# A retention and phase-mixing kernel: a new written-out order with 40 DMA transposes for 35, and output tiles in token-weight buffers

## The chip, the cores and the metric

The kernel runs on one core of a Trainium2 chip. The metric is device time in microseconds, lower is better. The core has TensorE (PE, matrix products, with PEld for its weight loads), VectorE (DVE), ScalarE (ACT), GpSimd (POOL) and SyncE (SP), which here only issues transfers. ACT issues some too.

## The reference

The first half is a recurrent retention over 4 batches, 8 heads, 768 tokens and head size 64; the second mixes the result over tokens with a learned phase. Cut to what is computed:

```
state = gamma[h] * state + outer(k[t], v[t])          # per batch and head
x[t]  = scale * q[t] @ state                          # heads side by side: [4, 768, 512]
theta = x @ w_theta
y     = w_tok_r @ (x * cos(theta)) + w_tok_i @ (x * sin(theta))
u     = x + y
out   = u + relu(u @ w_ch)
```

All inputs and the output are float32; the products are done in bf16.

## The kernel before

Tokens are taken in *units*: unit n is 256 tokens of one batch and four of the eight heads, so 24 units, six to a batch. A *chunk* C is 128 tokens with all heads: 24 chunks, six to a batch. An output *tile* t is 128 tokens of the output.

Nothing is scheduled by a compiler. The string ORDER (L23) lists every step, and each engine executes its own steps in the order in which they stand there. SP has one queue for nearly all transfers, also in order. A step that waits therefore holds all that is behind it on its engine. The last letter of a token names the engine (p POOL, v DVE, a ACT) or the issuing queue (s SP, a ACT).

Per unit n: Lk, Lq and Lv (L157) load k, q and v, 256 KB each, into nine rotating buffers per kind. ck (L275) casts k, cq (L278) scales q by its decay, cv (L282) scales v. Then k and q are transposed into kqT, either on PE (Tk and Tq, L293, copied out of PSUM by E, L302), or by one DMA transpose Dk (L307). G(n) on PE is three groups: A(n) (scores of unit n, L323), Y(n-1) (scores times v, L393) and ST(n) (the new part of the state, L351). m(n) on DVE (L330) masks the scores. SU(n) on DVE (L357) updates the state, SB(n,g) (L369) copies half of it to bf16, and I(n) on PE (L375) multiplies q by it. So G(n), SU(n), SB(n), I(n), G(n+1) is a chain, and I(n) also waits until XA(n-1) on ACT (L409) has read the previous result out of the one PSUM buffer R.

Per chunk C: x is put in token order by Tx on PE (L424, copied by Ex) or by a DMA transpose Dx (L433); Hh on PE (L438) gives theta, CN on ACT (L445) cosine and sine, z (L451) their products with x. z of the six chunks of a batch and the transposed token weights are what the token mixing M(t,s0) on PE (L483, twelve matmuls to a tile) needs. The token weights come as twelve rows: Lw loads (four buffers "wtok", L184), cw casts, Tw transposes on PE (L469), Ew copies. The weights of theta and of the channel product come by Lth and Lch and are cast in four parts (cth, cch).

Per tile t: u on DVE (L492) adds x; u is transposed on PE (Tu, L497, copied by Eu) or by DMA (Du, L508); O on PE (L512) is the channel product; f on DVE (L519) the rectifier and the sum, into one of four "ot" buffers; SO (L524) stores it. A buffer of "ot" is free again when its store has landed. The last tile is done in two halves (Mh, uh, Tuh, Oh, fh, SOh). warm(n) puts n matmuls on PE whose result nobody reads (L255).

Of the kernel before, what the change touches and what calls it, by code (L numbers as in the profile page):

```python
# [14 lines left out]
FT = mybir.dt.float32  # L15
# [17 lines left out]
I.4 CN.1.0 Tx.3 ck.6.a G.5 cq.6.v Tq.6 Lv.7.s Lk.8.s CN.1.1 Lq.8.s z.0.p SU.5 SB.5.1.p Tk.6
cw.1.0.p cv.6.p Lw.0.1.s m.5 Lv.8.s Ex.3.a XA.4.1 Hh.3 XA.4.0 ck.7.p Tx.2 cq.7.p Lk.9.s E.6.v
Lq.9.s Hh.2 Ex.2.v CN.3.0 ck.8.p SB.5.0.a z.1.v Lw.1.1.s Tw.1.0 Lv.9.s Ew.1.0.v CN.3.1 cq.8.p I.5
cv.7.p CN.2.0 z.3.v cv.8.p G.6 XA.5.1 Tk.7 XA.5.0 Hh.5 Lk.10.s Tq.7 Tk.8 CN.2.1 m.6 CN.5.1 Lq.10.s
CN.5.0 SU.6 Hh.4 E.7.v SB.6.1.a Tq.8 SB.6.0.a Tx.4 M.0.0 I.6 cw.0.1.a G.7 z.2.v E.8.v Ex.4.v Tx.5
SU.7 CN.4.1 Lw.0.2.s M.0.1 Ex.5.v ck.9.p CN.4.0 cq.9.p M.0.2 XA.6.0 Tw.0.1 SB.7.1.p XA.6.1
SB.7.0.a Lw.1.2.s m.7 z.4.v Tk.9 M.0.3 Tq.9 Ew.0.1.a cw.1.1.p I.7 Lv.10.s Lk.11.s G.8 XA.7.0
Lq.11.s z.5.v E.9.a cv.9.p Tw.1.1 M.0.4 Ew.1.1.v XA.7.1 Lw.0.3.s M.0.5 u.0 Lw.1.3.s SU.8 SB.8.0.v  # L40
Hh.6 ck.10.p cq.10.p cw.0.2.p m.8 Lw.0.4.s cw.1.2.p Tk.10 Lw.1.4.s M.1.0 Lv.11.s M.1.1 CN.6.0
cw.0.3.p M.1.2 M.1.3 Tq.10 SB.8.1.a I.8 M.1.4 Tw.0.2 M.1.5 E.10.v Lch.s cw.1.3.p Lk.12.s Lq.12.s
Ew.0.2.v Tw.1.2 CN.6.1 cv.11.p G.9 Ew.1.2.a ck.11.a Hh.7 u.1 M.2.0 ck.12.p XA.8.0 CN.7.0 CN.7.1
M.2.1 cq.11.v cq.12.p cv.10.v SU.9 Lv.12.s Lk.13.s Tk.11 XA.8.1 SB.9.1.v M.2.2 Tq.11 cv.12.p M.2.3
M.2.4 SB.9.0.v ck.13.p Tw.0.3 Dx.6 Lw.0.5.s Lw.1.5.s m.9 M.2.5 Dk.12 E.11.a Tw.1.3 I.9 Lq.13.s
Lv.13.s cw.0.5.p Ew.0.3.v G.10 Lk.14.s Lq.14.s Ew.1.3.a Tu.0 u.2 SU.10 Eu.0.v M.3.0 M.3.1
SB.10.0.a Tu.1 cw.0.4.a cw.1.4.v Lv.14.s Lk.15.s Eu.1.v SB.10.1.v M.3.2 XA.9.0 m.10 M.3.3 cch.3.v
Tx.7 XA.9.1 cq.13.p M.3.4 Ex.7.a M.3.5 Tw.1.4 I.10 Tw.0.4 cch.1.a cch.0.a Dk.13 G.11 Ew.1.4.v
cch.2.v u.3 Tu.2 O.0 SU.11 Ew.0.4.a ck.14.p Tu.3 cv.14.p XA.10.0 M.4.0 Eu.2.a m.11 M.4.1 f.0
Eu.3.v z.6.v M.4.2 M.4.3 Lq.15.s SB.11.0.a O.1 M.4.4 cq.14.p XA.10.1 SB.11.1.a M.4.5 Tw.0.5 f.1  # L50
Lv.15.s Tx.8 Hh.8 Lk.16.s cw.1.5.a Ew.0.5.v I.11 Tw.1.5 u.4 Ex.8.a G.12 Ew.1.5.v Tx.9 M.5.0
Lq.16.s cq.15.p SU.12 M.5.1 z.7.v Ex.9.v Dk.14 CN.8.1 CN.8.0 XA.11.1 Hh.9 SB.12.1.v CN.9.0 Lv.16.s
ck.16.p O.2 XA.11.0 CN.9.1 z.8.v M.5.2 f.2 Lk.17.s M.5.3 Tx.11 M.5.4 Lq.17.s Lv.17.s SB.12.0.a
SO.0.s Ex.11.a M.5.5 Tx.10 Lk.18.s Hh.10 SO.1.s Hh.11 z.9.v cv.13.v SO.2.s Lq.18.s CN.10.0 ck.15.p
Lv.18.s u.5 M.6.0 m.12 M.6.1 CN.10.1 M.6.2 cv.15.p CN.11.1 cq.16.p Ex.10.v I.12 G.13 CN.11.0 M.6.3
z.10.v Tu.5 XA.12.1 z.11.v Eu.5.a M.6.4 SU.13 M.6.5 SB.13.0.v O.3 u.6 Tu.4 M.7.0 ck.17.p M.7.1
# [12 lines left out]
M.12.3 Lv.22.s Ex.17.v CN.16.1 XA.18.1 CN.17.0 m.19 SB.19.1.a z.16.v CN.17.1 O.9 I.19 SO.6.s G.20
M.12.4 z.17.v M.12.5 f.9 Lk.23.s XA.19.1 Hh.19 Lq.23.s Dk.22 O.10 SU.20 Lv.23.s cv.22.p u.12  # L70
M.14.0 SB.20.0.a m.20 M.14.1 CN.19.0 ck.23.p M.14.2 SB.20.1.v M.14.3 M.14.4 XA.19.0 cv.21.v
cq.23.p M.14.5 I.20 f.10 G.21 O.11 u.14 M.16.0 M.16.1 SU.21 M.16.2 Dx.18 XA.20.1 SB.21.0.a cv.23.p
XA.20.0 M.16.3 M.16.4 M.16.5 SB.21.1.v f.11 CN.19.1 m.21 Hh.18 I.21 u.16 Dk.23 M.15.0 M.15.1 Dx.19
Du.12 CN.18.1 SO.9.a G.22 M.15.2 SU.22 XA.21.0 SB.22.0.v XA.21.1 m.22 M.15.3 M.15.4 Du.16 SO.8.s
M.15.5 CN.18.0 Dx.20 Hh.21 u.15 SB.22.1.p I.22 G.23 XA.22.1 z.18.v M.13.0 z.19.p M.13.1 SU.23 m.23
SO.10.a Hh.20 XA.22.0 SB.23.0.v Dx.21 M.13.2 Du.14 M.13.3 M.13.4 M.20.0 CN.20.1 M.20.1 CN.20.0
CN.21.1 SB.23.1.v O.16 I.23 G.24 XA.23.0 f.16 M.13.5 XA.23.1 CN.21.0 z.20.p O.12 Hh.23 M.22.0 f.12
Hh.22 M.22.1 Dx.22 z.21.p CN.23.0 u.13 Dx.23 M.18.0 CN.22.0 SO.11.s M.22.2 CN.22.1 Du.15 M.18.1
M.20.2 z.22.v M.22.3 CN.23.1 M.18.2 M.18.3 M.22.4 z.23.v O.14 M.20.3 M.22.5 f.14 M.18.4 M.18.5
Du.13 M.20.4 u.22 u.18 M.19.0 O.15 M.17.0 M.19.1 SO.16.a M.17.1 f.15 SO.14.s M.19.2 Du.22 M.19.3  # L80
M.17.2 M.17.3 O.13 f.13 M.17.4 M.17.5 u.17 M.19.4 SO.12.s Du.18 O.18 M.21.0 M.21.1 f.18 M.19.5
O.22 u.19 Du.17 M.21.2 M.21.3 f.22 SO.15.s M.21.4 Du.19 SO.13.a M.21.5 u.21 Du.21 O.17 M.20.5 f.17
Mh.0.0 u.20 Mh.0.1 Mh.1.0 Mh.0.2 Mh.0.3 SO.18.a Mh.0.4 Mh.0.5 uh.0 O.19 Tu.20 Mh.1.1 SO.22.s f.19
Mh.1.2 Eu.20.a Mh.1.3 Mh.1.4 Mh.1.5 uh.1 SO.17.s Tuh.0 O.20 Euh.0 f.20 Tuh.1 O.21 SO.19.s Euh.1
Oh.0 Oh.1 f.21 SO.20.a SO.21.a fh.0 SOh.0 fh.1 SOh.1
""".split()


# [11 lines left out]
def kernel(  # L100
# [14 lines left out]
    B, H, S, D = q.shape  # L115
    dm = H * D
    P = 128
# [10 lines left out]
    io = ctx.enter_context(tc.tile_pool(name="io", bufs=2))  # L128
    work = ctx.enter_context(tc.tile_pool(name="work", bufs=3))
# [131 lines left out]
    st = {}  # L261
# [255 lines left out]
        st["o", t] = o_ps  # L517

    def f(t):  # L519
        st["ot", t] = work.tile([P, dm], FT, name="ot", bufs=4)  # L520
        nc.vector.scalar_tensor_tensor(st["ot", t], st["o", t], 0.0, st["u", t], ALU.max,  # L521
                                       ALU.add)

# [86 lines left out]
```

## Time and profile before

| | us |
|---|---|
| median of three runs | 170.73 |
| lowest and highest | 168.94, 171.44 |
| the profiled execution | 170.49 |
| its span | 168.8 |
| PE busy, ACT busy, POOL busy | 156.0, 79.2, 78.5 |
| DVE busy | 123.8 |
| matmuls for x transposes on PE (L427) | 52 |
| matmuls for u transposes on PE (L500) | 36 |
| DMA transposes (Dk, Dx, Du) | 10, 11, 14 |
| their median time from issue to landing | 4.7, 3.4, 3.3 |
| stores issued by SP and by ACT (whole tiles) | 16, 7 |
| HBM read, written | 25.69 MB, 6.29 MB |

How to read it: the slices cut the span in 40 parts of 4.2 us and show each engine's busy share in tenths. The groups give, for a line, engine and operation, the count, the busy time, the mean of one in ns, and the idle time of the engine before them with what ended it. Matmuls are pipelined, so the busy time of one is longer than the distance between two starts. The waits of SP's queue are times in which SP could not issue its next transfer.

### The profile page before, as it was taken

To read this page: it belongs to the slowest core of one execution; us is meant where nothing else is said; L and a number is where in the kernel's file an instruction comes from. 1 tells how busy PE (TensorE), PEld (TensorE's weight loads), DVE (VectorE), ACT (ScalarE), POOL (GpSimd) and SP (SyncE) were. 2 spreads that over 40 slices of the span, in tenths; PEclk is the share of its full clock that TensorE was granted. 3 is DMA by queue.
4 is the path that set the end of the run, shared out by engine and by line. 5 is a ranking of instruction groups with operands and counts; after the bars stand their busy time and mean duration, and the time that the engine had idled before them with its cause. 6 is when DMAs were issued, how large, how long until landed. Compare 5 with 4: busy or idle time off the path is not lost.

```text
span 168.8 us, 4924 instructions
## 1 busy us (share of the span) xinstructions
PE 156.0 (92%) x2017; PEld 89.0 (53%) x2044; DVE 123.8 (73%) x200; ACT 79.2 (47%) x159; POOL 78.5 (47%) x99
## 2 busy tenths in 40 slices
PE   7988794989899989999999999999999999999991
PEld 2555463557566655555645565554555444444660
DVE  3497979699999897899669979689737443526552
ACT  6346385587657755666322593674323544000030
POOL 3778377998932634669203658023354560000000
PEclk9999999599999999999999999999999999999999
DMA  4999999999799999999999188899998736335555
GB/s 141 296 290 332 329 322 289 274 319 350 257 283 329 221 232 292 254 207 309 305 244 227 65 188 209 124 276 168 269 230 133 197 62 186 93 93 194 88 188 186
DMA packets 68582, 38.20 MB, mean 226 GB/s; under 512 B 25936, under 2 KB 63056, under 8 KB 68560
## 3 DMA queue, kind: packets, MB, share of 16 engines
q1 hardware_dynamic: 67408, 35.92, 88.8%
q10 hardware_dynamic: 1152, 1.97, 3.5%
q8 instruction: 16, 0.26, 0.6%
q14 instruction: 6, 0.05, 0.1%
HBM read 25.69 MB, written 6.29 MB: 189 GB/s over the span
## 4 chain that ended last, share of the span: by engine, by line
PE 65%; DVE 14%; SPq 11%; DMA 4%; issue 2%; ACT 1%; DVEq 0%; ACTq 0%
PE y_ps L488 31%; PE o_ps L515 11%; PE th_ps L441 9%; SPq L157 9%; DVE z L455 5%; DMA qf<-in_q_dram 4%; DVE at L332 3%; PE at_ps L323 3%; PE r_ps L393 2%; PE r_ps L380 2%; PE y_ps L538 2%; DVE kqb L279 1%; PE kq_ps L293 1%; PE w_ps L472 1%; SPq L185 1%
## 5 line engine op out<-in xcount | busy, mean ns | idle before, releaser
L488 PE MATMUL y_ps<-z,wtr 128*128 128x512 bf16 x135 | 51.2, 379 | 1.0 <-DVE z L455 0.5
L488 PE MATMUL y_ps<-z,wti 128*128 128x512 bf16 x129 | 48.9, 379 | 0.4 <-issue 0.3
L413 ACT CAST xT<-r_ps 128x256 bf16<-128x256 f32 x48 | 16.9, 372 | 30.7 <-PE r_ps L351 19.6
L279 POOL TENSOR_TENSOR kqb<-qf,qsc 128x512 bf16<-128x512 f32 x20 | 23.7, 1189 | 14.1 <-DMA qf<-in_q_dram 13.7
L332 DVE TENSOR_TENSOR at<-at_ps,mask 128x1024 bf16<-128x1024 f32 x24 | 29.1, 1213 | 1.1 <-PE at_ps L323 1.0
L521 DVE SCALAR_TENSOR_TENSOR ot<-o_ps,u 128x512 f32<-128x512 f32 x23 | 15.8, 689 | 14.9 <-PE o_ps L515 14.8
L441 PE MATMUL th_ps<-wth,xT 128*128 128x512 bf16 x89 | 25.0, 395 | 1.4 <-POOL wth L139 1.0
L285 POOL TENSOR_TENSOR vb<-vf,vsc 128x512 bf16<-128x512 f32 x17 | 18.9, 1114 | 10.0 <-DMA vf<-in_v_dram 9.9
L515 PE MATMUL o_ps<-wch,uT 128*128 128x512 bf16 x88 | 23.2, 379 | 0.4 <-DVE wch L139 0.2
L488 PEld LDWEIGHTS <-wti 128*128 128x128 bf16 x138 | 13.5, 98 | 13.4 <-issue 1.1
L448 ACT ACTIVATE cs<-th_ps,halfpi 128x512 bf16<-128x512 f32 x24 | 16.5, 688 | 8.2 <-PE th_ps L441 5.8
L488 PEld LDWEIGHTS <-wtr 128*128 128x128 bf16 x138 | 13.5, 98 | 13.0
L495 DVE TENSOR_TENSOR u<-y_ps,x_sb 128x512 bf16<-128x512 f32 x23 | 15.8, 686 | 5.8 <-PE y_ps L488 5.8
L448 ACT ACTIVATE cs<-th_ps,zerob 128x512 bf16<-128x512 f32 x24 | 16.2, 687 | 5.7 <-PE th_ps L441 5.3
L455 DVE TENSOR_TENSOR z<-cs,x_sb 128x1024 bf16<-128x1024 bf16 x18 | 16.6, 936 | 2.9 <-ACT cs L448 2.7
L455 POOL TENSOR_TENSOR z<-cs,x_sb 128x1024 bf16<-128x1024 bf16 x6 | 12.9, 2153 | 6.6 <-DMA x_sb<-xT 3.9
L139 POOL CAST kqb<-kf 128x512 bf16<-128x512 f32 x16 | 10.6, 666 | 8.3 <-DMA kf<-in_k_dram 6.1
L441 PEld LDWEIGHTS <-xT 128*128 128x128 bf16 x96 | 9.0, 100 | 10.3 <-issue 1.8
L515 PEld LDWEIGHTS <-uT 128*128 128x128 bf16 x92 | 8.7, 98 | 9.5 <-issue 0.3
L137 ACT COPY uT<-u_ps 128x512 bf16<-128x512 bf16 x6 | 3.5, 589 | 21.3 <-PE u_ps L500 21.3
L258 PE MATMUL y_ps<-zero 128*128 128x512 bf16 x36 | 12.0, 447 | 1.4 <-DVE zero L194 1.3
L293 PE MATMUL kq_ps<-ident,kqb 128*128 128x128 bf16 x112 | 9.8, 223 | 2.2 <-DVE kqb L279 2.2
(74 smaller groups left out, 209.3 us busy)
## 6 DMA issues: line engine op xcount, KB each, us to landing
kf<-in_k_dram SPq DMA_DIRECT2D x24, 256.0 KB, 5.4
qf<-in_q_dram SPq DMA_DIRECT2D x24, 256.0 KB, 5.1
vf<-in_v_dram SPq DMA_DIRECT2D x24, 256.0 KB, 5.4
out_dram<-ot SPq DMA_DIRECT2D x16, 256.0 KB, 3.3
wtok<-in_moe_w_tok_r_dram SPq DMA_DIRECT2D x6, 384.0 KB, 6.1
wtok<-in_moe_w_tok_i_dram SPq DMA_DIRECT2D x6, 384.0 KB, 5.9
out_dram<-ot ACTq DMA_DIRECT2D x7, 256.0 KB, 2.1
w<-in_moe_w_theta_dram SPq DMA_DIRECT2D x1, 1024.0 KB, 8.4
```

The source lines that it names most:

```text
L157: queues[e].dma_start(out=t.rearrange("p h a d -> p h (a d)"), in_=src[b, h * HU:(h + 1) * HU, i * 2 * P:(i + 1) * 2 * P, :].rearrange("h ...
L279: engines[e].tensor_mul(in_blocks(kqb_of(n)[:, 1]), by_token(raw["qf", n]), _bcast_last(K["qsc"][:, i, :, h * HU:(h + 1) * HU], D))
L285: engines[e].tensor_mul(in_blocks(vb), by_token(raw["vf", n]), _bcast_last(K["vsc"][:, i, :, h * HU:(h + 1) * HU], D))
L332: nc.vector.tensor_mul(at.rearrange("p g j a t -> p (g j) (a t)"), st["at_ps", n].rearrange("p g j a t -> p (g j) (a t)"), _bcast_mid(K["m ...
L413: nc.scalar.copy(st["xT", 2 * i + c][:, 2 * h:2 * h + 2].rearrange("p j (t a) -> p j t a", a=2), st["R", n + 1][:, c, :2 * P].rearrange("p ...
L441: nc.tensor.matmul(th_ps, st["xT", C][:, j, :], K["wth"][:, j, :], start=(j == 0), stop=(j == 3))
L448: nc.scalar.activation(st["cs", C][:, w, :], st["th_ps", C], AF.Sin, bias=K["zerob" if w else "halfpi"], scale=1.0)
L455: engines[e].tensor_mul(st["z", b][:, c], st["cs", C], _bcast_mid(x_of(C), 2))
L488: nc.tensor.matmul(st["y", t], K["wT"][r][:, s0, t0 * P:(t0 + 1) * P], st["z", b][:, s0, r, :], start=(s0 == 0 and r == 0), stop=(s0 == nT ...
L495: nc.vector.tensor_add(st["u", t], st["y", t], st["x", b][:, t0, :])
L515: nc.tensor.matmul(o_ps, st["uT", t][:, j, :], K["wch"][:, j, :], start=(j == 0), stop=(j == nD - 1))
L521: nc.vector.scalar_tensor_tensor(st["ot", t], st["o", t], 0.0, st["u", t], ALU.max, ALU.add)
```

## The change

The order is replaced as a whole. What it holds, by kind:

| step | before | after |
|---|---|---|
| Dk, Dx, Du (DMA transposes) | 10, 11, 14 | 10, 14, 16 |
| Tx, Tu (groups of four PE transposes) | 13, 9 | 10, 7 |
| Tk and Tq pairs on PE | 14 | 14 |
| warming matmuls | 40 | 43 |
| E on ACT, DVE | 6, 8 | 8, 6 |
| Ex on ACT, DVE | 5, 8 | 6, 4 |
| Eu on ACT, DVE | 6, 3 | 4, 3 |
| SB on ACT, DVE, POOL | 23, 18, 7 | 22, 13, 13 |
| ck on ACT, DVE, POOL | 5, 3, 16 | 9, 6, 9 |
| cq on DVE, POOL | 4, 20 | 2, 22 |
| cv on DVE, POOL | 7, 17 | 8, 16 |
| z on DVE, POOL | 18, 6 | 16, 8 |
| SO on SP, ACT | 16, 7 | 10, 13 |

DMA transposes are now Dk of units 11, 13, 14, 15, 18 to 23 (before 12, 13, 14, 16, 17, 19 to 23), Dx of chunks 6, 7, 10 and 13 to 23 (before 6, 13 to 16, 18 to 23), and Du of tiles 2, 3, 7 to 10, 12 to 19, 21, 22 (before 8 to 19, 21, 22).

The diff, cut to the stretches that are spoken of below; lines of the order are regrouped by stretch, and a lone "..." marks what is left out:

```diff
-Lk.4.s cq.3.p SU.1 ck.3.p Tq.2 E.2.a SB.1.1.a Lq.4.s
-Lth.s SB.1.0.v cv.3.p warm.7 I.1 G.2 Lv.4.s
...
-SU.2 cq.4.p cth.2.p SB.2.0.v SB.2.1.v Lk.5.s warm.2 Tk.4 Tq.4 Ex.1.v Lq.5.s Lw.0.0.s
-cth.1.a warm.2 I.2 E.4.v G.3 SU.3 XA.2.1 cth.0.p SB.3.1.a Tx.0 warm.3 Hh.0 SB.3.0.v cv.4.p XA.2.0
...
-I.4 CN.1.0 Tx.3 ck.6.a G.5 cq.6.v Tq.6 Lv.7.s
+Lv.4.s Lth.s warm.4 G.1 ck.3.a cq.2.v cq.3.p Tk.2 m.1 Tq.2 XA.0.0 E.2.a
...
+XA.1.0 XA.1.1 SB.2.1.v Tk.3 warm.7 I.2 cq.4.v Tx.1 cth.2.p cth.0.v E.3.a warm.2 G.3 Tk.4
+ck.5.p Lv.5.s cth.1.a cth.3.a Lk.6.s Ex.1.v Lw.0.0.s XA.2.0 SU.3 Tq.4 Tx.0 Hh.1 Hh.0 XA.2.1
+SB.3.0.p m.3 cq.5.p CN.1.1 cv.5.p SB.3.1.v E.4.v Lw.1.0.s Lq.6.s I.3 CN.1.0 CN.0.1 Lw.0.1.s Ex.0.a
+cw.0.0.p CN.0.0 z.1.v Tq.5 ck.6.v G.4 cq.6.p Lv.6.s XA.3.0 Tk.5 Lw.1.1.s Tx.2 Lk.7.s XA.3.1 SU.4
+SB.4.1.a m.4 Lq.7.s E.5.v cv.6.p cw.1.1.p cw.1.0.a Tw.0.0 Ex.2.a SB.4.0.v Lv.7.s Lk.8.s I.4
...
-Lv.14.s Lk.15.s Eu.1.v SB.10.1.v M.3.2 XA.9.0 m.10 M.3.3 cch.3.v
-Tx.7 XA.9.1 cq.13.p M.3.4 Ex.7.a
...
-SO.0.s Ex.11.a M.5.5 Tx.10 Lk.18.s Hh.10 SO.1.s Hh.11 z.9.v cv.13.v SO.2.s
...
+ck.10.v Eu.0.a G.9 Ew.1.3.v cch.3.p cch.1.v XA.8.0 m.9 CN.6.1 M.2.0 Dx.6 M.2.1 M.2.2 Lq.12.s
+M.2.3 Lw.0.4.s cch.0.v SU.9 SB.9.1.a cq.11.p M.2.4 M.2.5 Tq.10 Lw.1.4.s Tk.10 Dk.11 u.2 Tu.1
+Lw.0.5.s Dx.7 cv.10.v XA.8.1 O.0 SB.9.0.p M.3.0 cq.12.p M.3.1 E.10.v Lw.1.5.s ck.12.a cw.1.4.a
+cv.11.p Du.2 M.3.2 I.9 M.3.3 Eu.1.v f.0 M.3.4 Tk.12 Tq.12 cw.0.4.p M.3.5 G.10 cw.0.5.p u.3 Tw.0.4
+E.12.a Lv.12.s Ew.0.4.v Tw.1.4 Lk.13.s
...
+G.15 M.8.0 SO.0.a f.4
...
+SO.14.a u.21 M.20.3 O.17 Mh.0.0 f.17 M.20.4 Mh.0.1 Du.21 M.20.5 Mh.1.0 SO.22.s u.20 SO.17.a
+uh.0 O.19 Mh.1.1 f.19 SO.15.s Tu.20
...
     def f(t):
-        st["ot", t] = work.tile([P, dm], FT, name="ot", bufs=4)
+        if t >= 4 and (t < 8 or t % 2):
+            st["ot", t] = io.tile([P, S], FT, name="wtok", bufs=4)[:, :dm]
+        else:
+            st["ot", t] = work.tile([P, dm], FT, name="ot", bufs=4)
```

In f, tiles 4 to 7 and the odd tiles from 9 on now write their output into the first 512 columns of a buffer of the token weights; the others keep the four "ot" buffers. What each step computes is unchanged.

## The prediction

> **What bounds the kernel now.** I read busy shares and slices first, then five-microsecond windows, the timeline of the one hole, the groups of instructions, and the waits of SP's queue.
>
> ```profile
> span 168.8 us, 4924 instructions
> PE 156.0 (92%) x2017; PEld 89.0 (53%) x2044; DVE 123.8 (73%) x200; ACT 79.2 (47%) x159; POOL 78.5 (47%) x99
> ...
> PE   7988794989899989999999999999999999999991
> ...
> DVE  3497979699999897899669979689737443526552
> ...
> PEclk9999999599999999999999999999999999999999
> DMA  4999999999799999999999188899998736335555
> ```
>
> From slice 11 (46 us) on TensorE is full: what is ordered there is paid in full, except where something comes late. Ahead of that it has holes, and there DVE and DMA are near their limits. The windows show it (columns: PE, PEld, DVE, ACT, POOL busy, clock, DMA share):
>
> ```profile
> 25.00:30.00 5.00, 2.67 (x69) 1.90 (x69) 4.62 (x6) 2.68 (x6) 4.00 (x4) 0.98 1.12 290
> 30.00:35.00 5.00, 4.95 (x74) 3.21 (x74) 3.60 (x6) 2.92 (x7) 5.00 (x7) 0.68 1.01 287
> ...
> 45.00:50.00 5.00, 5.00 (x86) 3.31 (x86) 4.66 (x9) 2.63 (x5) 2.76 (x4) 1.00 0.71 221
> ```
>
> ```profile
> 26.32 2.40 DVE L279 TENSOR_TENSOR kqb<-qf,qsc 128x512 bf16<-128x512 f32 x1 [0.39 <-DMA qf<-in_q_dram]
> ```
>
> TensorE's largest hole ends at 28.8 us: q of unit 6 lands at 26.3, and DVE needs 2.40 us to scale it (0.68 at best) while POOL computes a z. After the hole the clock is at half for 3.4 us, which costs 1.7.
>
> ```profile
> L427 PE MATMUL x_ps<-ident,xT 128*128 128x128 bf16 x52 | 5.3, 227 | 0.9 <-DVE kqT L139 0.8
> L500 PE MATMUL u_ps<-ident,u 128*128 128x128 bf16 x36 | 3.5, 219 | 0.2 <-DVE wti L139 0.2
> L413 ACT CAST xT<-r_ps 128x256 bf16<-128x256 f32 x48 | 16.9, 372 | 30.7 <-PE r_ps L351 19.6 <-DVE s L365 6.7 <-DVE s L367 2.7
> ```
>
> Matmul durations overlap, so PE is priced by start-to-start times: four transposes 0.22 us, a pair of token matmuls (M) 0.43, a phase or channel product (Hh, O) 0.86, a weight row (Tw) 0.34, a G 0.70, a warming matmul 0.215.
>
> ```profile
> SPq L434 <- ACT xT L413: 6.4, 3, 5.1
> SPq L510 <- DVE u L495: 6.3, 3, 4.0
> ```
>
> SP issues in order; a transpose that waits for its source holds the loads behind it.
>
> **What the skill says.** "TensorE: Matmul & The Clock Gate", Part 1: the clock halves after about one idle window of 3.4 us and recovers after one busy window, windows running freely. The trace agrees on 3.4 us at half clock, but the hole before it was only 2.2 us. "GPSIMD Engine Reference", section 1: POOL shares its SBUF interfaces with VectorE, with contention for DVE instructions of two SBUF inputs; the 2.40 beside 0.68 agrees. "DMA: Bandwidth & Descriptors", Issuing engines are not separate DMA queues: moving stores to ACT saves issue time only; ACT's issue takes 0.34 to 0.39 us here when it isn't held up, a store on SP about 0.5.
>
> **The change, part by part.** (1) PE loses three Tx and two Tu groups: 5 x 0.22 = 1.1 us. Three warming matmuls are added (0.65), in the head, where PE mostly waits anyway; were that cover gone, they would cost those 0.65. Useful PE work goes from 140.3 to 139.2 us.
>
> (2) The five results go by DMA instead: Dx 11 to 14, Du 14 to 16, Dk stays 10 for other units. In the stream of landings a Dk adds 0.9 us, a Dx or Du about 0.45, a 256 KB load 0.9. So 5 x 0.45 = 2.3 us of the DMA stream, plus 1.2 us of SP per issue, 6 us. SP's loads are issued 4 to 5 us ahead of landing. Stores 0 to 2, which stood among the loads near 76 us, go out later (3 x 0.8 off the stream), so by q of unit 17 the streams are equal: I add 77.8 us against 78.8 before. The adding: landings follow one another from 4 us on, 0.9 apart, a 1 MB weight 3.9, a token row 1.1. Priced at nothing while the cover lasts, since PE has other ordered work meanwhile: v of unit 12 lands at 61.6 for its G near 66.8; Dk.13 about 69 to 71 for G.13 at 74; q of unit 16 at 74 for its transpose at 80. The cover is 3 to 5 us.
>
> (3) Other engines, by counts times row means: DVE loses about 6 us (E -2, Ex -4, SB -5, cq -2, z -2; ck +3, cv +1); POOL gains 4 (SB +6, z +2, cq +2, ck -7), ACT 3, and six more stores to issue (6 x 0.35 to 1.25). ACT sits at 47% and waits 30.7 us in the xT row, so nothing; without that cover its 3 us and the issues, up to 8, would count. POOL's copies of the state lie on SU, SB, I, G; POOL waited 13.9 us for DVE there, so nothing up to one long POOL operation (2.1) for each that queues behind one.
>
> (4) The head. Theta's load goes behind v of unit 4: it lands 0.9 later, at 20.6. One of its casts is put on DVE, a new wait; behind it on DVE stand Ex.1, SU.3, m.3, SB.3.1 and E.4, for which G.4 waits. By rows: 20.6 + 0.66 (cast) + 0.34 + 0.6 + 1.13 + 0.35 + 0.65 = 24.4 for G.4, against 22.35 before. Then z.1 0.9, ck.6 0.7, SU.4 0.6, m.4 1.15, E.5 0.6, SB.4.0 0.4 make I.4 28.85 (25.0 before). What PE has still to do decides: I summed the PE work from such points to the end of the order. From I.4 it is 129.8 in the new order; before, the latest such point was the transpose of unit 6: 28.78 + 130.0 = 158.8. After: 28.85 + 129.8 = 158.7. The hole is of the same length (about 2.4) at the same place, so I keep the half clock. Next, M.0.0 began at 37.97 with 123.5 left, sum 161.5; now the rows run on from I.4 to G.6 at 33.4 (PE, 3.3 of work, and DVE, Ew, z.0, SU.5, m.5, E.6, level), SU.6, z.3, E.7 and m.6 end at 37.4, G.7, Tx.5 and Tq.8 follow, and M.0.0 begins at 38.6 with 120.9 left: 159.5, with the half clock's 1.7 kept 161.2, 0.3 earlier. Of the waits later in the old order (0.48 for a z, some tenths for u and wch) I take 0.8 off for the lighter DVE (near 100% between 40 and 80 us); bounds 0 and 1.2.
>
> (5) The output tiles. f of tiles 4 to 7 and the odd ones after takes a token-weight buffer; these are free once the last cast row is read, before tile 4. Stores are late, so f waits for them: the closest are f.11 on SO.5, f.15 on SO.7 and f.21 on SO.15, issued 2.5 to 6 us of PE work ahead, with landings in 2.1 (ACT) and 3.3 us (SP). Nothing while that PE work covers them; without it, a landing time less the lead, 1 us at f.21 close to the end. In the tail the same last PE pieces and two half stores remain.
>
> **Sum.** 165.1 (last PE) less 0.3 less 0.8 = 164.0, that is -1.1 us. It agrees with the transposes' 1.1, which is in the 161.2 and not added again. The profiled execution took 170.49 us (span 168.8 and 1.7 around it), 0.2 under the median 170.73 of the runs: 169.4.
>
> **The rivals.** *A, the hole closes.* If the half clock does not come, 1.7 more is saved: 167.7. If also DVE is sooner with m.3 and half of the hole goes (1.2), 166.5. For: DVE no longer does cq.6 beside a z. Against: my chain leaves PE dry from 26.4 to 28.85, and a free-running window may even catch it worse.
>
> *B, slower: the SP queue.* The transposes of units 11 and 7 and tile 2 (Dk.11, Dx.7, Du.2) now stand ahead of v12 and k13, near 52 us; before, v12 and k13 had gone out at 49 and 51. If each waits for its source as the rows show (2 to 4 us in one wait) and DMA runs dry meanwhile, as it did near 46 us, the loads come later, one after the other. It decides from about 5 us of lateness: at 10, PE stands 5 us, less the 1.1: 174.4; with a half-clock period 176. For: the 35 transposes had some 40 us of SP waits in all. Against: u.2 is due about 53, q11 lands about 51, so I see a hold of 1 to 2 us.
>
> *C, the head slips.* DVE's chain behind theta has no slack. One operation stretched as the 2.40 was (+1.7) and a second half clock (+1.7): 169.4 + 3.4 = 172.8.
>
> *D, nothing moves:* PE gains are eaten by other waits, 170.5. That buffers or order fail to act is excluded for PE's own instructions, which stand in the order as written.
>
> **How the numbers follow.** About 2% (below 167.1, above 173.9) is what a measurement of this kernel can tell from no change. Forecast 0.40, A 0.19, B 0.20, C 0.13, D 0.08. A is past the 2% in its better half (0.10), B in 0.17 of its 0.20, C (172.8, with another stretched operation 174.5) in 0.07. Faster 0.10, same 0.66, slower 0.24. Range 166.5 (A at its best) to 175.0, which leaves out the worse part of B.
>
> **What would show it.** Right: 20 fewer transposes on PE; G.4 near 24.4 and I.4 near 28.9, later than before, with M.0.0 near 39 to 40; one half-clock period near 30; PE full from 46 us on; DVE about 118 us busy; q of unit 17 landed by 80. Wrong: PE waiting after 50 us for kqb, vb or kqT of a load or a DMA transpose (B); two half-clock slices (C); none (A); f waiting on an out_dram store in the last 30 us.

## The result, and the profile after

| | before | changed |
|---|---|---|
| median, lowest to highest (us) | 170.84, 168.94 to 171.44 (4 runs) | 176.61, 175.00 to 177.35 (4 runs) |
| ratio to before, 95% interval | | 1.0351 [1.0257, 1.0446] |
| profiled execution, its span | 170.49, 168.8 | 176.94, 175.0 |
| start of G.4, G.5, G.7 | 22.35, 25.83, 38.61 | 26.62, 31.96, 43.98 |
| start of M.0.0 | 37.97 | 45.45 |
| last PE instruction | 165.05 | 171.42 |
| half clock between 20 and 50 us | 3.4 | 10.2 |

The change costs 3.5%, where 169.4 was forecast; 176.6 lies above the range. Below, a ratio is always that to the kernel before on the same chip, from undisturbed runs; where there were too few of those (e1, e16, e17) the medians stand instead, and the profiled executions of e5, e14, e16 and e17 were disturbed ones, so little is read from their later parts.

The page of the changed kernel: busy times, then tenths of 40 slices of 4.4 us.

```profile
span 175.0 us, 4909 instructions
PE 157.7 (90%) x2000; PEld 89.5 (51%) x2027; DVE 115.1 (66%) x189; ACT 82.1 (47%) x162; POOL 80.0 (46%) x102
...
PE   7988755996899989999999979999999999999991
...
DVE  1487587649986988987786477667486443534553
...
PEclk9999995579999999999999999999999999999999
DMA  4999999999969989246999689897999689712285
```

PE has low digits (7, 5, 5 and then 6, 8) up to 48 us, and from there it is nearly as full as before. DVE is lighter by 8.7 us, more than the 6 us of the prediction's counts, and that bought nothing. The same windows as before (PE, PEld, DVE, ACT, POOL busy, clock, DMA share, GB/s):

```profile
25.00:30.00 5.00, 2.95 (x64) 2.53 (x65) 3.84 (x6) 3.07 (x7) 2.60 (x4) 0.66 1.11 338
30.00:35.00 5.00, 3.97 (x65) 3.10 (x66) 3.48 (x7) 2.77 (x7) 4.54 (x5) 0.50 1.07 277
...
40.00:45.00 5.00, 3.08 (x64) 1.79 (x63) 5.00 (x6) 3.52 (x8) 5.00 (x4) 1.00 1.05 383
45.00:50.00 5.00, 4.58 (x84) 3.13 (x85) 4.54 (x8) 3.17 (x8) 3.52 (x5) 1.00 1.15 289
```

From 40 to 45 us PE is 3.08 busy while DVE and POOL are both at 5.00: two full engines, and PE waits for them all the same.

To find where it is lost I keep a ledger: the start of G(n) plus the PE work that the order still holds from there, by the prediction's start-to-start prices. Within one kernel the sum only grows when PE loses time. Changed less before (the difference can fall, because the kernel before loses time too, between G.5 and G.6 above all), it stands at 0.0 at G.3 (154.6 both), 2.0 at G.4, 5.0 at G.5, 3.4 at G.6, 4.5 at G.7, 4.9 at G.9 (167.1 against 162.2) and 6.2 at G.23. So in this execution four fifths are lost between G.3 and G.9, that is in the head. The raw starts overstate the loss: of the 7.5 us between the two starts of M.0.0, 2.6 are PE work that the new order puts ahead of it (123.5 us of work left before, 120.9 now), and 4.9 are lost.

The timeline of DVE there (start, duration; in brackets the idle time before and what ended it):

```profile
21.19 0.43 DVE L139 CAST wth<-w 128x512 bf16<-128x512 f32 x1 [1.78 <-DMA w<-in_moe_w_theta_dram]
21.53 0.42 DVE L139 COPY x_sb<-x_ps 128x512 bf16<-128x512 bf16 x1
22.63 0.29 DVE L365 TENSOR_TENSOR s<-r_ps,s 128x128 f32<-128x128 f32 x1 [0.68 <-ACT xT L413]
...
23.16 1.22 DVE L332 TENSOR_TENSOR at<-at_ps,mask 128x1024 bf16<-128x1024 f32 x1
24.39 1.15 DVE L139 CAST sbd<-s 64x256 bf16<-64x256 f32 x1
25.57 0.69 DVE L139 COPY kqT<-kq_ps 128x1024 bf16<-128x1024 bf16 x1
...
28.69 0.29 DVE L365 TENSOR_TENSOR s<-r_ps,s 128x128 f32<-128x128 f32 x1 [1.10 <-ACT xT L413]
...
39.76 2.44 DVE L455 TENSOR_TENSOR z<-cs,x_sb 128x1024 bf16<-128x1024 bf16 x1
...
42.72 1.21 DVE L332 TENSOR_TENSOR at<-at_ps,mask 128x1024 bf16<-128x1024 f32 x1
```

The same steps in the kernel before (SU.3, SB.3.0, m.3 and SU.4):

```profile
19.27 0.29 DVE L365 TENSOR_TENSOR s<-r_ps,s 128x128 f32<-128x128 f32 x1 [0.16 <-PE r_ps L351]
...
19.80 0.27 DVE L139 CAST sbd<-s 64x256 bf16<-64x256 f32 x1
20.00 1.21 DVE L332 TENSOR_TENSOR at<-at_ps,mask 128x1024 bf16<-128x1024 f32 x1
...
23.46 0.28 DVE L365 TENSOR_TENSOR s<-r_ps,s 128x128 f32<-128x128 f32 x1
```

and of ACT in the changed kernel, which SU.3 waited for:

```profile
21.19 1.14 ACT L137 CAST wth<-w 128x512 bf16<-128x512 f32 x2 [2.28 <-DMA w<-in_moe_w_theta_dram]
22.23 0.36 ACT L413 CAST xT<-r_ps 128x256 bf16<-128x256 f32 x1
```

Theta lands at 21.16. The length of the cast on DVE (0.43) is not the trouble. SU.3 at 22.63 waits for an xT, and ACT makes that xT only after its own two theta casts. SU does not need xT: both read the PSUM buffer R, XA stands first in the new order, and the two reads run one after the other as written. Before, no XA stood ahead of SU.3 or SU.4; now one and two do. Then the 64x256 cast (SB.3.1) takes 1.15 us, where the one of the kernel before took 0.27, and later z takes 2.44. POOL beside the cast:

```profile
24.34 1.04 POOL L285 TENSOR_TENSOR vb<-vf,vsc 128x512 bf16<-128x512 f32 x1
```

The cast ends at 25.54, 0.16 us after this. On PE:

```profile
22.00 0.39 PE L427 MATMUL x_ps<-ident,xT 128*128 128x128 bf16 x4 [0.93 <-DVE x_sb L139]
...
25.64 0.38 PE L380 MATMUL r_ps<-kqT,sbd 128*128 128x128 bf16 x4 [1.52 <-POOL vb L285]
...
26.62 0.64 PE L323 MATMUL at_ps<-kqT 64*64 64x128 bf16 x16
...
30.81 0.80 PE L472 MATMUL w_ps<-ident,wrow 128*128 128x128 bf16 x6 [1.93 <-ACT x_sb L137]
```

Transposes wait for the copies that empty their PSUM buffers (two, "tr", shared by all transposes on PE): Tx.0 for Ex.1, Tw.0.0 for E.5, which ends at 30.71 (the view names Ex.2, which ends at 30.76 but empties the other buffer). The 1.52 is put down to a vb that I.3 (L380) does not read; what I.3 reads, sbd, is made until 25.54.

From there to G.23 the ledger gives 1.3 us more: v of unit 10 on DVE took 3.25 us, and I.16 stood 1.11 us behind a queue on POOL:

```profile
59.55 3.25 DVE L285 TENSOR_TENSOR vb<-vf,vsc 128x512 bf16<-128x512 f32 x1
```

```profile
102.97 0.40 PE L380 MATMUL r_ps<-kqT,sbd 128*128 128x128 bf16 x4 [1.11 <-POOL sbd L139]
```

### The profile page after: what moved, and what is told of

It is laid out like the page before. It is cut to its first block, busy times and chain, and to the rows that moved or that the text cites. A ratio compares the mean times of both kernels' runs of the same rounds, so it can differ in the third digit from the quotient of the medians.

```text
span 175.0 us, 4909 instructions
## 1 busy us (share of the span) xinstructions
PE 157.7 (90%) x2000; PEld 89.5 (51%) x2027; DVE 115.1 (66%) x189; ACT 82.1 (47%) x162; POOL 80.0 (46%) x102
## 4 chain that ended last, share of the span: by engine, by line
PE 61%; DVE 8%; DMA 3%; SPq 3%; POOL 3%; issue 2%; ACT 1%; DVEq 0%; POOLq 0%; ACTq 0%
PE y_ps L488 27%; PE o_ps L515 9%; PE th_ps L441 9%; DMA out_dram<-ot 3%; PE at_ps L323 3%; PE w_ps L472 3%; PE r_ps L393 2%; PE r_ps L380 2%; DVE vb L285 2%; PE y_ps L541 1%; PE kq_ps L293 1%; DVE z L455 1%; DVE at L332 1%; POOL vb L285 1%; DVE kqT L139 1%
## 5 line engine op out<-in xcount | busy, mean ns | idle before, releaser
L488 PE MATMUL y_ps<-z,wtr 128*128 128x512 bf16 x131 | 49.8, 380 | 0.4
L285 POOL TENSOR_TENSOR vb<-vf,vsc 128x512 bf16<-128x512 f32 x16 | 17.0, 1062 | 12.9 <-DMA vf<-in_v_dram 10.0
L455 POOL TENSOR_TENSOR z<-cs,x_sb 128x1024 bf16<-128x1024 bf16 x8 | 16.9, 2124 | 11.3 <-DMA x_sb<-xT 5.9
L455 DVE TENSOR_TENSOR z<-cs,x_sb 128x1024 bf16<-128x1024 bf16 x16 | 13.0, 827 | 3.3 <-ACT cs L448 2.7
L258 PE MATMUL y_ps<-zero 128*128 128x512 bf16 x40 | 12.7, 440 | 1.4 <-DVE zero L194 1.3
L137 ACT COPY uT<-u_ps 128x512 bf16<-128x512 bf16 x4 | 2.3, 586 | 24.8 <-PE u_ps L500 24.8
L524 DVE SCALAR_TENSOR_TENSOR ot<-o_ps,u 128x512 f32<-128x512 f32 x12 | 8.2, 687 | 8.6 <-PE o_ps L515 7.2
L137 ACT COPY kqT<-kq_ps 128x1024 bf16<-128x1024 bf16 x8 | 8.1, 1015 | 11.0 <-PE kq_ps L293 11.0
L285 DVE TENSOR_TENSOR vb<-vf,vsc 128x512 bf16<-128x512 f32 x8 | 8.5, 1058 | 5.4 <-DMA vf<-in_v_dram 5.2
```

The lines of the kernel that those rows point to most:

```text
L137: nc.scalar.copy(dst, src)
L258: nc.tensor.matmul(t, K["zero"][:, :P], K["zero"], start=True, stop=True)
L285: engines[e].tensor_mul(in_blocks(vb), by_token(raw["vf", n]), _bcast_last(K["vsc"][:, i, :, h * HU:(h + 1) * HU], D))
L455: engines[e].tensor_mul(st["z", b][:, c], st["cs", C], _bcast_mid(x_of(C), 2))
L488: nc.tensor.matmul(st["y", t], K["wT"][r][:, s0, t0 * P:(t0 + 1) * P], st["z", b][:, s0, r, :], start=(s0 == 0 and r == 0), stop=(s0 == nT ...
```

## The experiments

In the diffs a minus is the changed kernel's order (of e7 and e8, the order of the kernel before) and a plus the experiment's.

### Head or rest: e1, e2

e1 takes the old order up to M.0.0 and the new one from there; e2 the other way round.

```diff
 e1, up to M.0.0:
-... ck.5.p Lv.5.s cth.1.a cth.3.a Lk.6.s Ex.1.v Lw.0.0.s XA.2.0 SU.3 Tq.4 Tx.0 Hh.1 Hh.0 XA.2.1 ...
+... cth.1.a warm.2 I.2 E.4.v G.3 SU.3 XA.2.1 cth.0.p SB.3.1.a Tx.0 warm.3 Hh.0 SB.3.0.v cv.4.p XA.2.0 ...
```

> The old order up to the copy Ex.4 just after M.0.0 and G.7, then what is left of the new order. If the loss is made ahead of M.0.0 (head theory): M.0.0 near 38 us, one half-clock period of 3.4 us, and 170 to 172.5 us in all, within 2 us of the kernel before. If the loss is made by the transfers that the new order puts on SP's queue, or by the store buffers (queue theory): 175 to 177, as the changed kernel.

> The new order up to M.0.0, then what is left of the old order, with the old output buffers. Head theory: M.0.0 near 45 us, three half-clock periods, 174.5 to 176.5 us. Queue theory: 170 to 172, as the kernel before.

e1: 171.63 us (170.23 to 173.16) beside 170.32, M.0.0 at 36.99, last PE 165.07. e2: ratio 1.0404 [1.0158, 1.0649], M.0.0 at 42.61. With the old head, and all 40 DMA transposes and the new store buffers behind it, most of the loss is gone (0.8% is left at the medians); with the new head it is there whole. e2's profile has no half clock after the start at all:

```profile
PEclk9999999999999999999999999999999999999998
```

and still begins M.0.0 4.6 us later than the kernel before. Of these, 1.7 are work that stands ahead of M.0.0 now, and 2.9 are lost; 4.5 are lost at the end. The order of the head makes the loss, and it does so without any half clock.

### The clock: e3, e7, e8

e3 puts warming matmuls into the new head's holes; e7 takes 32 of the 40 out of the kernel before, e8 fills the hole of the kernel before (the cosine of chunk 1 is moved up there too).

```diff
 e3
-Hh.0 XA.2.1
+Hh.0 warm.4 XA.2.1
-Tx.2 Lk.7.s
+Tx.2 warm.8 Lk.7.s
 e7, as in ten places
-warm.7 I.1
+I.1
 e8
-G.5 cq.6.v
+G.5 CN.1.1 warm.8 cq.6.v
```

> The changed kernel with four warming matmuls more after Hh.0 and eight after Tx.2, where PE stood for 1.5 and 1.9 us ahead of and in the half-clock periods. If the half clock is what makes the holes dear (clock part of the head theory): half-clock time falls from 10.2 us to 3.4 or less and the time by 2 to 3.5 us, to 173 to 174.5. If PE only waits for DVE, POOL and DMA there and the clock matters little: 176 to 177.5.

> The kernel before without its 32 warming matmuls after the first eight; nothing of the result hangs on them. It prices the clock by itself. If a half clock in the head costs as much as the difference asks (3 us for two periods more): half-clock time of 10 us or more from 8 to 30 us, and 173 to 176 us. If the clock costs little because PE waits for DVE and DMA in the head anyway: 170 to 171.5, in spite of 10 us or more at half clock.

> The kernel before with eight warming matmuls in its hole of 2.2 us ahead of Tq.6. If the one half-clock period costs its full 1.7 us: no half clock near 30 us and 168.3 to 169.3. If the stretch behind the hole is bound by DVE: half clock gone, time within 0.7 us of the kernel before.

e3: 1.0324 [1.0091, 1.0557], no half clock after the start, M.0.0 at 42.2. Its median is 1.7 us under the changed kernel's, which its interval doesn't resolve. e7: 1.0095 [1.0055, 1.0135], with 10.2 us at half clock in its profile:

```profile
PEclk9955799999999999999999999999999999999999
```

e8: 0.9998 [0.9967, 1.0028], with none. So ten microseconds at half clock, from 9.0 to 19.3 us and with 32 warming matmuls fewer, cost the old order 1%. The changed kernel's lie later, from 26.6 to 36.8, so this is no price of those. In the kernel before the half clock did slow PE where it stood: PE was busy there (4.95 of the 5 us from 30 on), and in e8, without it, M.0.0 begins at 36.37, 1.6 us sooner. But the ledger of e8, 1.5 us better than before at G.9, is only 0.3 better at the end: later waits take the lead back. In the changed kernel the other three runs had a mean clock of 0.978 to 0.981 against 0.971 in the profiled one, so some 7 us at half clock by an estimate (twice the missing share of the span), and took 175.0 to 177.35 us beside its 176.94: no gain that shows.

### The queue of transposes: e6

Five of the new DMA transposes go back to PE (Dx.7, 10, 17 and Du.2, 3), 35 in all again.

```diff
-Dx.7
+Tx.7 Ex.7.a
-Du.2
+Tu.2 Eu.2.a
```

> The changed kernel with the five added DMA transposes (chunks 7, 10, 17 and tiles 2, 3) back on PE with copies on ACT and DVE: 35 DMA transposes as before, PE 1.1 us more. Queue theory (these transposes hold the loads behind them): 2 us or more faster, 174.5 or less. Head theory: they are off the path, and the time rises by 0 to 1.5 us, 176.5 to 178.

1.0626 [1.0464, 1.0788], slower than the changed kernel. What it loses against the changed kernel is one step of 5.06 us in the ledger at G.10. Most of it is here, and 3.4 us at half clock follow:

```profile
58.27 0.38 PE L426 MATMUL x_ps<-ident,xT 128*128 128x128 bf16 x4 [3.11 <-DVE kqT L138]
```

This PE transpose stands where its buffer isn't free yet, and all of PE waits behind it. So e6 is no clean price of a transpose, and it can't decide about the SP queue. e1 can: it keeps the 40 DMA transposes, and most of the loss is gone. What the queue still does to a kernel with the new head is said below, with e15 and e16.

### Theta's casts: e4, e5, e11, e12

e4 puts the cast on DVE on POOL. e5 puts all but POOL's cast behind m.3, e11 theta's load ahead of v of unit 4, and e12 clears the whole stretch for G.4: SU.3, SB.3.0, m.3, SB.3.1, E.4 ahead of all casts, the phase products behind G.4.

```diff
 e4
-cth.0.v
+cth.0.p
 e5
-Tx.0 Hh.1 Hh.0 XA.2.1
+Tx.0 XA.2.1 m.3 cth.1.a cth.3.a cth.0.v Hh.1 Hh.0
 e11
-Lv.4.s Lth.s
+Lth.s Lv.4.s
 e12
-cth.2.p cth.0.v E.3.a ... cth.1.a cth.3.a ... XA.2.0 SU.3 Tq.4 Tx.0 Hh.1 Hh.0 XA.2.1 SB.3.0.p m.3 ... SB.3.1.v E.4.v ... I.3 ... G.4
+SU.3 XA.2.0 Tq.4 Tx.0 XA.2.1 SB.3.0.p ck.5.p m.3 SB.3.1.v E.4.v cth.2.p cq.5.p cth.1.a cth.3.a cth.0.v ... I.3 ... G.4 SU.4 Hh.1 Hh.0
```

> The changed kernel with one theta cast (cth.0) on POOL and not on DVE. If DVE's new wait for theta starts the slip: Ex.1 runs before 20 us, Tx.0 at about 20.9 and not at 22.0, m.3 a little sooner, M.0.0 1 us sooner or more, time 1 to 3 us less (173.5 to 175.5). If m.3 is held by ACT's theta casts ahead of XA.2.0 all the same: m.3 stays at about 23 and the time within 1 us of 176.6.

> The changed kernel with the three theta casts of DVE and ACT put behind m.3 and XA.2 on their engines. If the wait for theta in the queues of DVE and ACT starts the slip: m.3 runs near 21 us and not at 23.2, G.4 starts by 25.5 (26.6 in the changed kernel), M.0.0 comes 2 us or more sooner (43.5 or less), and the time is 1.5 to 4 us less (172.5 to 175). If the slip comes from the casts being needed by Hh.1 and Hh.0 ahead of I.3 on PE, whoever does them: G.4 stays at 26 or later and the time within 1 us of 176.6.

> The changed kernel with theta's load ahead of v of unit 4, as in the old order. Theory theta: theta lands 0.9 us sooner, near 20.3, so Ex.1, the first phase products, ACT's casts, m.3 and G.4 are each 0.7 to 0.9 sooner (G.4 25.8, G.5 31.1), M.0.0 near 44.5, and the time is about 0.9 lower, 175.7. Rival, the chain behind it (the buffer R, POOL beside DVE) alone decides: G.4 moves by less than 0.3 and the time not at all, 176.6. v of unit 4 is needed for G.5 only and lands 0.9 later without cost in both.

> The changed kernel with the steps between G.3 and XA.3.0 put in another order: the copies and the mask for G.4 (SU.3, SB.3.0, m.3, SB.3.1, E.4) ahead of all four casts of theta on their engines, SU.3 and SU.4 ahead of XA.2.0 and XA.3.0, and the phase products of chunks 1 and 0 behind G.4 on PE, with the casts of v and w behind them. Theory, the three together make the head: G.4 near 24, G.5 27.5 to 28 (before 25.83), M.0.0 38 to 42, time 171 to 174. Rival, the head has a cause not named yet (clock, landings, transposes of tokens): G.5 at 30 or later, M.0.0 at 43 or later, time 175 to 177.

e4: 1.0438 [1.0308, 1.0568]; m.3 at 22.36 instead of 23.16, G.4 at 25.82. e5: 1.040 [1.0189, 1.0611]; m.3 at 21.50, but G.4 at 27.39, because the phase products, which need the casts, stand ahead of I.3 on PE:

```profile
23.44 1.57 PE L440 MATMUL th_ps<-wth,xT 128*128 128x512 bf16 x4 [2.19 <-DVE wth L138]
```

e11: 1.0359 [1.0287, 1.0431]; G.4 at 26.07, G.5 at 31.01, all sooner, and the time the same. e12: 1.0572 [1.0476, 1.0668]; G.4 at 25.15, but z.1 on DVE, ahead of m.4, now waited 2.74 us for cosines that come after the late phase products, and G.5 began at 34.89. None of the four made the kernel measurably faster: each shortens one branch of the knot and another one holds. Theta's landing alone is not the cause.

### The reads of R: e9

```diff
-XA.2.0 SU.3
+SU.3 XA.2.0
-XA.3.0 Tk.5 Lw.1.1.s Tx.2 Lk.7.s XA.3.1 SU.4
+SU.4 XA.3.0 Tk.5 Lw.1.1.s Tx.2 Lk.7.s XA.3.1
```

> The changed kernel with two steps moved: SU.3 stands ahead of XA.2.0 and SU.4 ahead of XA.3.0, as in the old order. Theory R: the two readers of the PSUM buffer R, DVE's state update and ACT's copies, go one after the other in the written order, so behind ACT's copies SU.3 lost 0.68 us and SU.4 1.10. Then those two waits for xT are gone; m.3 starts near 22.5 instead of 23.16 and m.4 0.7 to 1.7 sooner, G.5 near 30.5 to 31 instead of 31.96, and the time is 1 to 2 us lower, 174.5 to 175.5. Rival, theta: the chain of m.3 hangs on theta's landing at 21.16 and on what DVE does behind it; then the waits move to another partner, G.5 stays within 0.5 us, and the time stays at 176 to 177.

1.0254 [1.0183, 1.0325]; m.3 at 22.30, m.4 at 27.38 (28.90), G.5 at 29.88, M.0.0 at 41.13, no half clock after the start. DVE in e9:

```profile
21.78 0.28 DVE L364 TENSOR_TENSOR s<-r_ps,s 128x128 f32<-128x128 f32 x1
...
22.30 1.22 DVE L331 TENSOR_TENSOR at<-at_ps,mask 128x1024 bf16<-128x1024 f32 x1
23.53 1.66 DVE L138 CAST sbd<-s 64x256 bf16<-64x256 f32 x1
25.21 0.69 DVE L138 COPY kqT<-kq_ps 128x1024 bf16<-128x1024 bf16 x1
```

```profile
22.99 1.04 POOL L278 TENSOR_TENSOR kqb<-qf,qsc 128x512 bf16<-128x512 f32 x1
24.00 1.04 POOL L284 TENSOR_TENSOR vb<-vf,vsc 128x512 bf16<-128x512 f32 x1
```

SU.3 runs at once, 0.85 us sooner, and m.3 with it. But the gain at G.4 is only 0.35, because the cast behind m.3 now takes 1.66 us. POOL computes from 22.99 to 25.04 without a break, and the DVE cast comes to its end 0.15 after that. Not all of the time saved up to M.0.0 (4.3 us) is the swap's: e3, with the changed kernel's order of these reads and no half clock either, has G.5 at 30.99 and M.0.0 at 42.20, and beside that e9 is 1.1 us sooner at both.

### DVE beside POOL: e10

```diff
-z.2.p
+z.2.v
```

> The changed kernel with z of chunk 2 on DVE instead of POOL. Theory contention: POOL's 2.12 us z at 39.5 stretches DVE's z beside it from 0.83 to 2.44 us and with it m.6 and G.7. Then no DVE z near 40 us takes over 1.3, the step of the ledger at G.7 goes from 2.1 to 1 or less although DVE has 0.83 more to do, and the time is about 1 us lower, 175.5. Rival, the load of DVE itself: G.7 stays or is later by up to 0.8, and the time is 176.5 to 177.5.

1.0315 [1.0236, 1.0393], too near the changed kernel's to be told from it; in the trace the step of the ledger at G.7 is 0.40 instead of 2.11, although DVE has one z more (by M.0.0 1.4 us are lost again, beside 0.4 in the changed kernel: Tx.5 waited 0.90 for a copy that stands behind the added z):

```profile
38.86 0.72 DVE L454 TENSOR_TENSOR z<-cs,x_sb 128x1024 bf16<-128x1024 bf16 x1
```

The Trainium skill, "SBUF — State Buffer", section "Who interferes with whom", says that DVE and POOL share one pair of SBUF ports. A DVE cast or copy can run in a mode that takes this pair, and then whichever engine starts first has it for its whole instruction while the other is blocked; a DVE operation with two inputs in SBUF contends with POOL's reads. The traces agree: in the changed kernel POOL's z runs from 39.52 for 2.12 us, and DVE's z, begun at 39.76, ends at 42.20, that is 0.56 after POOL's end (0.72 is its length in e10). That z came in between two POOL instructions, and POOL's next one took 1.49 us instead of 1.04:

```profile
41.61 1.49 POOL L279 TENSOR_TENSOR kqb<-qf,qsc 128x512 bf16<-128x512 f32 x1
```

In other places DVE did not come in between: the cast of e9 ended only after the second POOL operation, and v of unit 10 (59.55, 3.25 us) only after three that began behind it, the last of which ended at 62.26. What decides between the two is not shown.

### The repairs together: e13, e14, e17, e18

e13 is e9, e10 and e11 together. e14 adds SB.3.1 on ACT ahead of its cosines, e17 puts z.1 and the cast of k of unit 6 behind m.4, E.5 and SB.4.0, and e18 adds six warming matmuls.

```diff
 e14
-CN.1.1 cv.5.p SB.3.1.v E.4.v
+SB.3.1.a CN.1.1 cv.5.p E.4.v
 e17
-z.1.v Tq.5 ck.6.v G.4 ... SB.4.1.a m.4 Lq.7.s E.5.v ... SB.4.0.v
+Tq.5 G.4 ... SB.4.1.a m.4 Lq.7.s E.5.v ... SB.4.0.v z.1.v ck.6.v
 e18
-Tx.2
+Tx.2 warm.6
```

> The changed kernel with the edits of e9, e10 and e11 together: state updates of units 3 and 4 ahead of ACT's copies, z of chunk 2 on DVE, theta's load ahead of v of unit 4. Theory, the named waits add up: G.5 near 29.3, no step above 1.0 in the ledger at G.7, M.0.0 near 39.5 to 40, sum at G.9 about 161.5 (162.2 before, 167.1 changed), and the time lower than in e9, ratio to before 1.01 to 1.02, because the z on POOL at 140 us then takes back 2 us. Rival, one cause behind them all: nothing beyond e9, M.0.0 at 41, ratio 1.025.

> e13 with one more edit: the copy SB.3.1 on ACT ahead of its cosines, where in e9 it took 1.66 us on DVE beside three operations of POOL. Theory contention: SB.3.1 takes 0.40 on ACT, E.4 follows m.3 at 23.5 to 24.2, G.4 near 24.8 instead of 26.3, G.5 near 28.5, M.0.0 near 38.5 to 39, sum at G.9 about 160.5; the time goes down by up to 1 us against e13, less if a later wait takes it back. Rival: G.4 waits for q of unit 5 and its scaling on POOL (24.0) anyway, so G.4 is at 25.5 or later and nothing is gained.

> e14 with two steps of DVE moved: z of chunk 1 and the cast of k of unit 6 behind m.4, E.5 and SB.4.0 instead of ahead of SU.4. Theory, they are the rest of the head's loss: m.4 at 25.5 instead of 26.75, G.5 28.0 to 28.5 instead of 29.76, M.0.0 at 40 to 41, sum at G.9 161.5 to 162.5, ratio to before 1.00 to 1.01. Rival: m.5 waits for z.1, z.0 and the q of unit 6 (lands at 27.1) anyway, so G.6 stays at 35 to 36, M.0.0 at 42, and the ratio stays at 1.01 to 1.02.

> e17 with six warming matmuls (1.3 us of TensorE work) behind the transposes of chunk 2, where TensorE waits. Theory clock: no half-clock period after 26 us, M.0.0 0.5 to 1.5 us sooner than in e17, the time 0.5 to 1.7 us lower. Rival: the clock is worth little once other waits follow, time within 0.5 us of e17.

| | G.4 | G.5 | M.0.0 | ledger at G.9 | last PE | ratio |
|---|---|---|---|---|---|---|
| before | 22.35 | 25.83 | 37.97 | 162.2 | 165.05 | 1 |
| changed | 26.62 | 31.96 | 45.45 | 167.1 | 171.42 | 1.0351 [1.0257, 1.0446] |
| e9 | 26.27 | 29.88 | 41.13 | 162.8 | 169.38 | 1.0254 [1.0183, 1.0325] |
| e13 | 24.27 | 29.04 | 41.86 | 163.2 | 168.85 | 1.0162 [1.0041, 1.0283] |
| e14 | 24.50 | 29.76 | 42.69 | 163.8 | 168.99 | 1.0103 [0.9972, 1.0235] |
| e17 | 24.45 | 28.58 | 42.07 | 164.8 | 171.37 | none; 172.13 beside 170.28 us |
| e18 | 24.27 | 27.98 | 39.22 | 160.5 | 166.18 | 1.0050 [1.0010, 1.0090] |

The ratios go down with each set of repairs. Neighbouring intervals overlap, so what each is worth alone isn't settled. Those of the changed kernel and of e18 do not: together the repairs take back 3.0 of the 3.5%. With the head repaired G.9 stands 1.7 us better than before in the ledger. But e8, the kernel before without its half clock, has 160.7 there, so beside that the repaired head is level with the old one, and no gain of the transposes shows. Single expectations failed: e13 hoped for M.0.0 at 39.5 to 40, and a stretched DVE z (1.53 us at 38.93) ahead of a copy cost 2.4 at G.8; in e14 the copy on ACT brought nothing at G.4, which stands where q of unit 5 and its scaling let it. e17's mask came as forecast (25.55) and G.5 nearly (28.58), M.0.0 not. e18 has no half clock. Its one large step from there is at G.20:

```profile
112.37 0.38 PE L487 MATMUL y_ps<-z,wtr 128*128 128x512 bf16 x1 [1.82 <-POOL z L454]
```

```profile
109.21 1.04 POOL L278 TENSOR_TENSOR kqb<-qf,qsc 128x512 bf16<-128x512 f32 x1 [4.21 <-DMA qf<-in_q_dram]
110.21 2.11 POOL L454 TENSOR_TENSOR z<-cs,x_sb 128x1024 bf16<-128x1024 bf16 x1
```

A z of chunk 14 stands on POOL behind the scaling of q of unit 21, and that q lands at 109.07: when PE is early, the next late thing is a landing. Moving that z ahead was not tried.

### What takes a lead back, and the output tiles: e15, e16

e15 is e14 with z of chunk 20 on DVE and its product two places later. e16 is the changed kernel with six "ot" buffers.

```diff
 e15
-M.22.0 z.20.p ... M.22.1 M.22.2 ... M.18.0 M.18.1
+M.22.0 z.20.v ... M.22.1 ... M.18.0 M.18.1 M.22.2
 e16
-            st["ot", t] = work.tile([P, dm], FT, name="ot", bufs=4)
+            st["ot", t] = work.tile([P, dm], FT, name="ot", bufs=6)
```

> e14 with two more edits late in the order: z of chunk 20 on DVE instead of POOL, and the token product M.22.2 that uses it two products later. Theory, that wait takes back what the head gives: TensorE's wait for a POOL z near 140 us (2.1 us in e9) is gone, and the time is 1.5 to 2.5 us lower than e14, at or below the kernel before (ratio 0.99 to 1.005). Rival, the new order's rest is bound elsewhere (landings, stores): the wait is found at another instruction after 110 us and the time stays within 0.7 us of e14.

> The changed kernel with six buffers of output tiles instead of four, nothing else. Theory, the buffers cost nothing since other TensorE work covers them: f of tile 10 no longer waits 1.4 us for the store of tile 1, and the time is unchanged, 176 to 177 beside 170.8 (ratio 1.03 to 1.04). Rival, the late stores have a part in the loss: the time is 1 to 1.5 us lower (ratio 1.025 to 1.03).

e15: 1.0255 [1.0163, 1.0346], a miss. There is no wait for that z (2.12 us in e9, but none over 0.3 in e14's own profile), and others stand in its place: 1.02 us of PE behind a copy on POOL, and 1.23 behind an f that itself waited 2.60 us for a store.

e16: 176.26 us beside 170.69, but three runs took 175.5 to 177.1 and one 171.63, so the time doesn't settle what the stores cost. The traces say this much: no f of e16 waits for a store, and in the changed kernel, where f of tile 10 waits 1.42 us for one, no PE wait follows. So in that execution the stores have no part in the loss. Where PE came earlier they had: 0.78 us of PE in e4 and the 1.23 in e15 stand behind that f.

The head of e16 is the changed kernel's, with 3.4 us at half clock instead of 10.2, and it began M.0.0 at 43.01. So of the 4.9 us lost ahead of M.0.0 in the changed kernel's profile, half (2.4) goes with that one execution: 0.75 of it stands at G.4 already, before any half clock, and the rest came while the clock was halved.

But PE does not keep this to the end. Less the kernel before, the ledger of e16 stands at 2.4 at G.9 and at 5.0 at the end, that of e4 at 2.4 and 5.8. What PE has in hand at G.9 is lost behind it, and a part of that is the SP queue: q of unit 16 lands late, and PE waits for its scaling. In e4:

```profile
84.98 1.10 POOL L278 TENSOR_TENSOR kqb<-qf,qsc 128x512 bf16<-128x512 f32 x1 [4.11 <-DMA qf<-in_q_dram]
```

```profile
86.14 0.40 PE L292 MATMUL kq_ps<-ident,kqb 128*128 128x128 bf16 x4 [1.03 <-POOL kqb L278]
```

The same wait is in e16 (1.15), e14 (1.09), e17 (0.83), e13 (0.82), e9 (0.68), e11 (0.65) and e18 (0.60). With the old head (e1) that q lands at 79.5 instead of 85.5 and PE doesn't wait for it: the queue's lateness comes with the new head.

## Why the prediction was wrong

**Step (1), PE's work:** right, though the 1.1 us less of it did not reach the time. 68 transposes for x and u are left of 88.

**Step (2), the SP queue:** right for this kernel that it does not bind, wrong in its landings. q of unit 16 was to land at 74 and landed at 85.5, q of unit 17 by 80 and at 90.9, v of unit 12 at 64.5 instead of 61.6. In the changed kernel's profile no PE wait over 0.3 us after 50 us names a load or a DMA transpose. That was luck as much as cover: PE was late itself. Its transpose of q of unit 16 came at 87.44, 0.7 us after POOL had scaled it, and in eight experiments that brought PE there sooner it waited 0.60 to 1.15 us. Rival B, which ended slower by this road, is not what made the loss (e1), but its queue takes back part of a better head.

**Step (3), the other engines:** DVE's 115.1 us is near the 118 forecast. "ACT, so nothing" is wrong: ACT's theta casts held XA.2.0, and SU.3 behind it. POOL, costed at nothing up to one long operation, was dear in another way, by blocking DVE.

**Step (4), the head:** this is the step that failed. Forecast and measured: G.4 24.4 and 26.62, I.4 28.85 and 31.40, M.0.0 38.6 and 45.45. (The terms as written add up to 24.33 and 28.68; this slip is small and on the safe side.) The terms were DVE durations alone in a row. Missing were: 0.68 and 1.10 us of SU behind ACT's copies out of R (without them e9 is about 1% lower, an unsettled figure: the intervals overlap); DVE operations stretched beside POOL (1.15 for a term of 0.35; later 2.44; e10 shows the mechanism, not its share of the time); Tx and Tw waiting for PSUM copies (0.93, 1.93); the cast of theta itself, at 21.16 instead of 20.6. Later theta alone (e11) cost nothing measurable, and how the loss divides among these terms stays open. The prediction had a 2.40 us DVE operation quoted in front of it and put such a thing into a rival instead of into the sum.

"I keep the half clock" (1.7 us) came out as 10.2 us at half clock, but this is not what made the kernel slow: e2 is slow with none. Nor does its absence pay as rival A had it: in e8 it is gone, and the time is the same. The 0.8 us of relief for a lighter DVE did not come.

**Step (5), the tiles:** nothing on PE, as said, though the f that waited (1.42 us for the store of tile 1) was that of tile 10, not 11, 15 or 21. Here too PE's lateness helped: in e4 and e15 that f held PE.

**Rival C**, the head slips, named the place and one of the mechanisms, with 172.8 us for one stretched operation and a second half clock. Several links slipped, and its chance of 0.13 was too small for a chain "without slack".

## What to carry to other kernels

In an order written out by hand, check for each buffer in what order its readers stand: the two engines that read one PSUM buffer here took turns as written (0.68 and 1.10 us of waiting), so a step on the critical chain belongs ahead of the one that can wait. Price the operations on such a chain by what runs beside them on the engine that shares their ports. When a saving on a full engine is at stake, ask first whether the stretch before it, where that engine waits, moves. And follow a lead to the end: here one of 1.5 us was down to 0.3 there (e8), while a delay of 4.1 us at G.9 was still 4.5 (e2).

## What the hardware showed that was not expected

A DVE operation beside POOL sometimes waited for several POOL instructions in a row (a cast of 0.27 us in the kernel before took 1.66 in e9, a product of 0.69 took 3.25), and sometimes came in after the first, and then POOL's next one was longer (1.49 us instead of 1.04). DVE operations that read PSUM kept their length there: the mask took 1.21 us at 42.72, with POOL busy all the time.

The clock halved for 3.4 us in one execution and for 10.2 in another, with the same order (e16 and the changed kernel). The same hole of 2.14 us ahead of Tw.0.0 was followed by half clock in e4 and by none in e2. "TensorE: Matmul & The Clock Gate", Part 1 of the Trainium skill, says that the windows by which the clock is set run freely, and this fits. Ten microseconds at half clock early in the old order cost 1% (e7).
